# Sketched attention and four attention experts on one core: a new order for 1,270 jobs, the last group projected expert by expert

## The chip, the cores and the metric

One core of one Trainium2 chip runs the whole kernel in one launch. The metric is device time in microseconds (us). The engines are TensorE (PE, with its weight loads shown as PEld), VectorE (DVE), ScalarE (ACT), GpSimd (POOL) and SyncE (SP, which here only issues DMAs). Each has its own instruction queue, worked in program order; they meet through semaphores.

## The reference

Two blocks follow each other. The first is attention through sketches: for 4 batches, 4 heads, 1088 rows and 32 columns per head,

```
phi(x) = outer(S1 x, S2 x)                 # 8 x 8 = 64 features per row
kv = sum over rows of phi(k) v^T,  z = sum over rows of phi(k)
x  = phi(q) kv / (phi(q) z + 1e-6)         # joined over heads: 1088 x 128 per batch
```

The second is a mixture of four causal attention experts on x, two of which are chosen per row:

```
logits = x @ w_gate;  the two largest of 4 are kept, their softmax gives the shares w
for each expert e:  q, k, v = x wq[e], x wk[e], x wv[e]
                    a  = softmax(causal(q k^T / 8));  ye = a v wo[e]
out = sum over the two chosen experts of w * ye        # 4 x 1088 x 128, float32
```

## The kernel before

The weights are folded once: Mq[e] = wq[e] wk[e]^T / 8 and Mo[e] = wv[e] wo[e]. Then a row's scores are (x Mq[e]) x^T, and the output is (a x) Mo[e], so keys and values are x itself.

Each batch is prepared (`prepare`): k, q and v are loaded, k and q are turned in 32x32 blocks on DVE, multiplied with the sketch matrices on PE (L518), turned back on DVE (L522), and multiplied feature by feature on DVE or POOL (L527). PE sums features times v (L558, "sums"). Batch 0 goes by rows (`attend_rows`): its query features are transposed on PE (L592, "turn qf"), copied to SBUF ("keep qf"), multiplied with the sums (L615, "numer"), divided on DVE, and turned into xT. The other batches stay turned (`attend_turned`, L757). `choose_experts` computes logits (L807), compares them on DVE (L832 and on), and makes masks and shares; the masks of the first group of batch 0 are widened on PE (L906), all others go through DRAM (mb<-md). x goes through DRAM as well and comes back as rows (xra, xrb, xrc).

A batch's 1088 queries, twice over for their two chosen experts, are 17 tiles of 128 (64 queries x 2), in three groups of 6, 6 and 5 tiles. For a group: `queries` multiplies x with the four Mq (L960), and DVE picks the chosen expert's columns (L973). `scores` computes a tile's scores (L998, "score"), DVE masks and takes the maximum (L1010, "take"), ACT takes the exponential (L1026), POOL multiplies with share and inverse sum (L1041, "weigh"), and DVE turns the tile (L1046, "turn A"). `values` sums rows of x with these (L1074, "sum"), copies the sums ("keep V"), patches in the queries whose expert stands second (L1097, "patch"), and POOL multiplies two experts at a time with their masks (L1101, "spread V"). `outputs` projects with Mo (L1144; for groups of 5 tiles turned, L1124, with a turn-back on DVE, L1127), copies and stores. Batches 0 to 2 take their groups in the order 0, 1, 2, the last batch 1, 2, 0: the last group of the kernel is group 0 of batch 3.

What each engine does when is no loop order. Every step is a job with a name and one or two engines that may run it. The list `ORDER` names all jobs by number, with a letter where there is a choice of engine; `Plan.run` emits the jobs in that order and gives each buffer (a PSUM pair, a tile of a pool) to the job that asks first. So `ORDER` fixes every queue and every buffer. The costs and landing times in the job definitions were for whoever made the list: they change no instruction. Idle matmuls ("dummy", L247) are 40 jobs that may be emitted on PE, two matmuls each, or left out.

At the start the queues hold, before the change:

```
SP    w_gate, load S0, q, q, k, k, then v (4 pieces and 1 small), k of batch 1 (4), q of batch 1, the weights
ACT   q, load S1, q, the table, spread2, keep qf (5), keep sums (2), keep x
POOL  ident, mask, pick8, const, spread1, gate order, features q (2), spread v1, spread v0, features k of batch 1, rep4, ..., onehot, rep16
DVE   decode, spread3, turn q (2), turn k (2), back q (2), features q (2), back k (2), features k (4), turn k of batch 1, ...
PE    4 dummies, sketch q0, sketch k0, dummy, turn qf (5), sums 0 (2), sketch k1, numer (3), turn x, turn w (3), logits, ...
```

Of the kernel before, what the change touches and what calls it, by code (L numbers as in the profile page):

```python
# [14 lines left out]
ALU = mybir.AluOpType  # L15
# [6 lines left out]
56 45 47 0 1 8a 77 60 46 3 2 76 25a 19a 17a 48 79 49 51 78 57 90 89 74 87 75 88 50 13b 98 100 99 102a 103a 91 92 83 93  # L22
97a 84 81 104b 22a 101b 113 96a 117 118a 82 111 112a 115 109 110a 94a 95a 38b 80 392 86 85 106 116a 393 114a 105 108a
107a 391 394 402 395 401 405 406 119 404 408a 54 120 124 125 129 407 130 121 66 122a 52 64 58 53 65 146 131 410a 126
411a 67b 132a 400 127a 147 152 55 68 397 396 69 123 71 150 70 148 153 155 44b 398 180 72 27b 16b 684 149 151 167 168
169 170 63 156 157a 158 685 159a 59 409b 179 184a 183a 154 162 163 181 399 185 73 182 413 412 186 414a 61 403 174 687
686 695 694 416 194 62a 415 417 195 196 420b 418b 215 216 419b 217 218a 421 222 423 9b 24b 31b 26b 422 164 219 171 128
165 137 187 188 133 172 246 173 430 431 197a 198 223 424 425 189 190a 191 245 250a 12b 166a 199 688 249a 201 202 200
318 5b 432 160 203 208 175 251 7a 426 427a 433a 224 247 192 428b 248 225a 161a 209 429 434a 210 252 319 322a 323a 193
435 698 268 226 227 700 699 204a 205 206 139 220 135 176 267 269 270 228 436 438a 207 141 703a 271b 704b 437b 324 221  # L30
211a 212 260 261 262 263a 213 275 321 276 277 278 279b 177 178b 214 253 254 456 458 272 457 273 14b 142 693 320 325
255 292 291 293 274 701a 42b 264 691 280 702a 134 136 229 230 231 459 460 692 256b 234a 284 294 283 233a 462 281 257
232a 258 265 690 689 706 705 285 286 235b 342 707a 708 237 236 239 709 710 696 713a 238 711a 712a 259 282 697 461 266
295a 296 343 326 344 297 287a 327 328 288 289 298 714 715 717 463 350 290 329 330b 716 723 724 725 345 346a 10b 143
21b 472 138 331 473 477b 718 347 351 352 35b 353 354a 144 727a 332 348 719 140 29b 439 476b 464 299 300 301 302 303
304 308a 441 306a 307a 726a 333 349 467 478 335 310 474 440 334 305b 309 475 336 479 359 337 338a 358 360 339 361 362
355 468 508 509 442 720a 984 311 312 540 721a 363 340 501 364a 443 502 480 979 341 481 482 541 314 465 487 365 488 356
357 483a 315 313 366 367 538 494 977 978 495 980 316a 981 728 539 542a 368 369 370 987 496 503 504a 145 371 372 373
374 317 469 375 470 543a 544 545 471a 505 506 985 988 484 485 486 497b 444 498 722 499 510 511b 489 490a 491 512 513
376 379b 447 500 380a 515 383 516 553 377a 381 445 554 492 493 378a 382 448 584 585 586 517 518a 729 555 449 446 453  # L40
982 983 730a 514 519 731b 451 991 520 521 993 749 556b 992 994b 587 588a 569 546 996b 750 384 385 997a 507 557 558 547
751 548 386 568 989 522 589 523 524 549a 550 551 559 570 571 526a 752 753 590 242 591 525a 754 611 529 995a 530 241
528b 527a 531 612 616a 561 760 732 452 387 615a 755 455 466 733 572a 756 560 573 574 389 614 562 563 986 613 240 576
577 617 618 620 575 43b 552 532 644 28b 18b 619 578 579 621 243a 580b 581 643 765 652 564a 565 766 769a 582 651 768
757 645 583 636 566 567 390 653 770a 771 635 654 655 627 622 244 623a 761 762 628 637 656 657b 629 630 638 767 772 624
658 659 646 625 592 660 639a 640 631b 641 593 594 450 595 596 597 794 598a 999 647a 632 642 601b 602 648 600a 599a 795
633 634 649 998 736 1000a 603 605 535 626 454 773 774 787 650 534 763 788 533 780 781 808 809 810 811a 764a 536b 812
661 662 789 775 663 813 796 797b 798 790b 604 782 664 665 666 667 1002 814 668 669 990 1005a 734 776b 777 672a 671a
778 1006b 670b 1001 735 739 1003 832 1004a 791 388 799 783b 800 673a 674 675 831 835a 801 784 1007 802 803 1008 792
676 1009 793 836a 834 677 1010 1016 833 904 738 678 742 30b 758 804b 1011 837 1017 785 805 806 759 1012 1018 838 1013a  # L50
905 908a 862 1014a 1020a 909a 807 679 910 878 786 779 737 537 877 879 747 839 840 841 907 906 880 911 861 863 1019a
1021 881b 842a 846 847 682 740 815 816 817 746 864 865a 820a 853 866 867 821a 824 854 1015 868 882 936 819a 823 39b
34b 40b 41b 855 848 849b 937 818a 850 851 856 822 938 1022 1024b 869 1023b 607 843 883 884 939 870 748 871 872 1042
857b 1044 928 680 741 681 844 845 1043 858 606 873a 874 929 608 1045 825 1047 852 930 940a 1046 1048 875 859 860 921
944 945 946 920 743 941 609a 922 610 744 913 931 932a 1049 912 914 947 933 934 942 915 948 876 949 950b 1126 916a 917
951 1125 1053 918 1054 1124 1128b 935 1025 1127 923 952 885 886 943 887 888 889 890 1129a 1051 891a 1130 1131 892b
924a 925 894b 895 828 896 926 898 893a 33b 927 32b 826 953 827 1139 829a 830 4 1147 1140 919 897 1055 1146 1132 1133
1148 1154 1155 1156 1198 1199 1149 1150a 1197 1201a 1134 1052 1027 1141 1142b 1143 1200 954 955 956 957 958 959 1202a
745 1029 1028 1026 1035 683 1037 960 1056 1057b 1135b 1157 1158b 1159 961 962 1203 1204 1213 1136 1137 1170 963a 1144
1145 1160 966a 1161 1171 1214 964a 968 1151 1152 1138 965a 967 1237 1205 1206 1172 1173 1174a 1238 1229 1215 970 969  # L60
1031 1207 1208 1209a 1239 1216 1059 1153 1039 1230 1162 1163 1217a 1240 1058 1231 1164 1061 1210 1211 1165 1241 1060
1063b 1050 1218 1062b 1166b 971 1064 1167 1175 1232 1242 899 1212 972 1168 1065 1176 1177 6b 1233a 1234 1169 1221
1243b 1040 1244 1222 1223 901 1235 1224 1066 900 1038 1067 1068 1245 1246 1219 1033 1069b 902a 1032 1030 1220 1101
1102 973 1178 1179 1034 1087 1225b 1226 1227 1236 1073 1074 1180 1075 1228 1088 1076a 1036 1181 1080 1081 1077 1094
1095 1096 1182 1103 1104b 1183 1184b 1097b 1098 1186b 1089 1090b 1091 1247 1248 1249 976 1187a 1105 1106 1250 1251
1252 1041 1188 1253 1254 1255 1185b 1189 1092 11b 1190 23b 903 1107 36b 1191 1194 1078 1070 1082 1083a 1193 1099 1093
975 1084 1071 1257b 1100 974 1192 1258a 1256a 1079 1085 1260 1261 1263 1259b 1086 1262 1072 1108 1195a 1196 1109 1110
# [47 lines left out]
def kernel(  # L115
# [14 lines left out]
    nc = tc.nc  # L130
# [188 lines left out]
    def spread(e, h):  # L319
        copy(e, SK[32 * h : 32 * h + 32], SK[0:32])  # L320
# [913 lines left out]
```

## Time and profile before

| | us |
|---|---|
| median of 3 runs | 279.85 (279.17 to 280.01) |
| the profiled execution | 280.91 |
| its span | 279.2 |
| TensorE busy | 263.8 |
| VectorE busy | 218.8 |
| GpSimd busy | 153.3 |
| ScalarE busy | 100.2 |
| mean granted TensorE clock | 0.994 |

A matmul's end in the profile is modelled, and a pair of matmuls in float32 counts as two instructions, so a full PE row is not PE at its peak. The idle time of an engine counts only where the chain of work that ended last passes through it.

### The profile page before, as it was taken

Reading aid. Unit: us, or ns where it says so; the run is one execution under the profiler, and the core shown is the slowest. Engines: PE = TensorE matmul, PEld = TensorE weight load, DVE = VectorE, ACT = ScalarE, POOL = GpSimd, SP = SyncE. Lnnn points to the kernel's source line nnn. Section 1 sums busy time; section 2 is a strip of 40 time slices with the busy share of each in tenths; the row PEclk is TensorE's granted clock in tenths of the full one; section 3 lists DMA queues with packets and bytes.
Section 4 is the critical chain, followed back from the end, with each engine's and each line's share of the span. In section 5 each row is a group of like instructions: output and inputs, shape, how many; then the busy total and the mean of one; then the engine's idle time right before and its main releaser. Section 6 shows DMA issues by size and latency. Waiting matters only on the chain.

```text
span 279.2 us, 9471 instructions
## 1 busy us (share of the span) xinstructions
PE 263.8 (94%) x3953; PEld 194.8 (70%) x3953; DVE 218.8 (78%) x541; ACT 100.2 (36%) x272; POOL 153.3 (55%) x246
## 2 busy tenths in 40 slices
PE   5789899899999999989999999999999999999993
PEld 1478575448486796676589976756696975789973
DVE  4895998999989987998969437999898468986340
ACT  2030346254333444433462331463423335233110
POOL 6323636677789834546565458655447432544570
PEclk9979999999999999999999999999999999999999
DMA  8855749921617879243900166701403756820012
GB/s 179 139 141 102 112 124 258 153 34 24 143 32 120 166 184 180 57 102 65 198 6 4 30 150 141 162 2 38 108 2 76 130 116 133 165 56 5 2 31 52
DMA packets 85547, 27.36 MB, mean 98 GB/s; under 512 B 54080, under 2 KB 84864, under 8 KB 85504
## 3 DMA queue, kind: packets, MB, share of 16 engines
q1 hardware_dynamic: 83280, 26.47, 46.4%
q8 instruction: 31, 0.51, 0.8%
q10 hardware_dynamic: 2224, 0.28, 0.6%
q14 instruction: 12, 0.10, 0.1%
HBM read 22.22 MB, written 4.52 MB: 96 GB/s over the span
## 4 chain that ended last, share of the span: by engine, by line
PE 70%; DVE 20%; issue 5%; POOL 2%; ACT 1%; DMA 1%; DVEq 0%; POOLq 0%
PE pair L1074 24%; PE pair L998 19%; PE pair L960 9%; PE pair L1144 6%; PE pair L518 3%; PE pair L558 3%; DVE AT L1046 2%; DVE w L522 2%; DVE w L1010 2%; DVE fp L527 2%; PE pair L1124 2%; PE pair L615 1%; PE pair L592 1%; DVE in L494 1%; DVE xT L191 1%
## 5 line engine op out<-in xcount | busy, mean ns | idle before, releaser
L1041 POOL TENSOR_SCALAR w<-w,rs,sh 128x384 f32<-128x384 f32 (+15 forms) x68 | 55.6, 824 | 54.8 <-DVE rs L1037 52.0
L998 PE MATMUL pair<-xT,qs 128*128 128x384 f32 (+11 forms) x216 | 76.8, 482 | 1.7 <-DVE agg L191 1.3
L1026 ACT ACTIVATE w<-w,mx 128x640 f32<-128x640 f32 (+15 forms) x68 | 52.4, 770 | 72.3 <-DVE mx L1010 56.6
L998 PEld LDWEIGHTS pair<-xT,qs 128*128 128x128 f32 x216 | 37.7, 190 | 26.9 <-issue 10.0
L1046 DVE STREAM_TRANSPOSE AT<-w 128x576 f32<-128x576 f32 (+13 forms) x68 | 50.6, 758 | 5.4 <-POOL w L1041 5.2
L1010 DVE CUSTOM_DVE_ANT_0 w<-pair,mask 128x768 f32<-128x768 f32 (+13 forms) x68 | 48.3, 721 | 5.4 <-PE pair L998 4.7
L1074 PEld LDWEIGHTS pair<-AT,xra 32*128 32x128 f32 x1136 | 41.6, 185 | 6.0 <-DVE mx L1010 2.6
L1074 PE MATMUL pair<-AT,xra 32*128 32x192 f32 (+5 forms) x1136 | 44.5, 303 | 0.0
L1101 POOL TENSOR_TENSOR agg<-agg,mb 128x768 f32<-128x768 f32 (+1 forms) x24 | 37.3, 1565 | 12.7 <-ACT agg L191 6.6
L960 PE MATMUL pair<-xT,Mq 128*128 128x384 f32 (+1 forms) x96 | 34.9, 478 | 0.1
L527 POOL TENSOR_TENSOR fp<-w 128x576 f32<-128x576 f32 x21 | 25.4, 1224 | 14.2 <-DVE w L522 12.5
L191 ACT COPY agg<-pair 128x384 f32<-128x384 f32 (+1 forms) x33 | 14.0, 462 | 44.2 <-PE pair L1074 37.7
L1074 PE MATMUL pair<-AT,xrb 32*128 32x160 f32 (+5 forms) x752 | 26.9, 287 | 0.3 <-issue 0.3
L1074 PEld LDWEIGHTS pair<-AT,xrb 32*128 32x128 f32 x752 | 26.1, 186 | 1.0 <-issue 1.0
L1144 PEld LDWEIGHTS pair<-Mo,agg 128*128 128x128 f32 x192 | 23.4, 192 | 4.1 <-POOL agg L1101 1.7
L1144 PE MATMUL pair<-Mo,agg 128*128 128x128 f32 x192 | 24.9, 279 | 1.0 <-POOL agg L1101 0.9
L960 PEld LDWEIGHTS pair<-xT,Mq 128*128 128x128 f32 x96 | 17.2, 190 | 11.2 <-issue 3.2
L973 DVE COPY_PREDICATED qs<-mb,pair 128x768 f32<-128x768 uint16 (+1 forms) x24 | 23.0, 960 | 2.4 <-DMA mb<-md 1.8
L191 DVE COPY agg<-pair 128x384 f32<-128x384 f32 (+1 forms) x15 | 7.9, 532 | 13.1 <-PE pair L1074 11.7
L518 PE MATMUL pair<-in,SK 32*32 32x288 f32 x416 | 13.4, 494 | 3.0 <-DVE in L494 3.0
L522 DVE STREAM_TRANSPOSE w<-pair 128x576 f32<-128x576 f32 x16 | 11.6, 756 | 5.6 <-PE pair L518 5.6
L1097 DVE COPY_PREDICATED agg<-mb,pair 128x384 f32<-128x384 uint16 (+1 forms) x24 | 12.6, 550 | 3.3 <-ACT agg L191 2.9
(160 smaller groups left out, 295.4 us busy)
## 6 DMA issues: line engine op xcount, KB each, us to landing
mb<-md SPq DMA_DIRECT2D x7, 576.0 KB, 5.2
xra<-xd SPq DMA_DIRECT2D x16, 192.0 KB, 4.3
xrb<-xd SPq DMA_DIRECT2D x16, 192.0 KB, 3.6
xrc<-xd SPq DMA_DIRECT2D x16, 160.0 KB, 4.9
mb<-md SPq DMA_DIRECT2D x4, 480.0 KB, 5.4
in<-in_k_dram SPq DMA_DIRECT2D x12, 136.0 KB, 4.1
in<-in_q_dram SPq DMA_DIRECT2D x3, 544.0 KB, 5.5
xd<-w SPq DMA_DIRECT2D x12, 136.0 KB, 3.5
```

The source lines that it names most:

```text
L191: (nc.scalar.copy if eng == "ACT" else VEC[eng].tensor_copy)(o, i)
L527: VEC[e].tensor_tensor(out=f, in0=a[:, :, None, R : 2 * R].to_broadcast([128, NJ, R, R]), in1=a[:, :, 0:R, None].to_broadcast([128, NJ, R, ...
L960: nc.tensor.matmul(plan[ps[x]][:, y, 0:w], Mq[:, ((1, 2), (0, 3))[x][y]], plan[xT][:, 64 * t0 : 64 * t1], start=True, stop=True)
L973: nc.vector.copy_predicated(chosen(), rows(c), rows(plan[ps[x]]))
L998: nc.tensor.matmul(plan[p][:, y, 0 : c1 - c0], plan[qs][:, 128 * t : 128 * t + 128], plan[xT][:, c0:c1], start=True, stop=True)
L1010: nc.vector.tensor_tensor_reduce(out=o, in0=src, in1=msk, scale=-1.0, scalar=mx[:, b, i, x - 1 : x] if x else 3e38, op0=ALU.add, op1=ALU.m ...
L1026: nc.scalar.activation(out=a, in_=a, func=ACTF.Exp, bias=mx[:, b, i, last : last + 1], scale=-1.0, accum_out=zs[:, b, i : i + 1])
L1041: nc.gpsimd.tensor_scalar(out=a, in0=a, scalar1=rs[:, b, i : i + 1], scalar2=plan[("sh", b)][:, i : i + 1], op0=ALU.mult, op1=ALU.mult)
L1046: nc.vector.transpose(dst[:, 0 : keys // 32, t], plan[A][:, 0:keys].rearrange("p (j s) -> p j s", s=32))
L1074: nc.tensor.matmul(plan[Vk[g // 2]][:, g % 2, lo : 32 * nt], plan[(f"xr{j // 12}", b)][rows, j % 12], a[rows, j, lo:], start=(j == 0), sto ...
L1101: nc.gpsimd.tensor_tensor(out=a, in0=a, in1=plan[mb][:, 2 * x : 2 * x + 2, 0:w], op=ALU.mult)
L1144: nc.tensor.matmul(plan[p][0:m, 0, 128 * x : 128 * x + 128], plan[agg][:, e, 128 * x : 128 * x + m], Mo[:, e], start=(e == 0), stop=(e == ...
```

## The change

1. `spread v` (the copy that brings batch 0's v into its padded tile) may run on ScalarE or POOL. In the new order the small piece (v1, 64x128) runs on ScalarE and the large one (v0, 128x1024) stays on POOL.
2. `spread2` on ScalarE follows the table load.
3. The last group (batch 3, group 0) has its own way in `values` and `outputs`: experts 0 and 1 are multiplied with their masks straight from PSUM on DVE ("mix"), experts 2 and 3 are kept, patched, and scaled one by one on POOL or DVE ("scale"), PE projects expert by expert as they come (order 0, 2, 1, 3) into three pieces in two PSUM pairs, and each piece is copied and stored by itself.
4. Nine dummies stand ahead of the first sketch instead of four; the two later ones are gone, and one stands behind the last projection.
5. All jobs have a new order. At the start:

```
SP    q, load S0, q, k, v, k, w, v, w, w, v, v, v small, k of batch 1, wo, w_gate, k of batch 1 (3), q of batch 1
ACT   load S1, q, q, the table, spread2, spread v1, keep w, keep qf (3), keep x, ...
POOL  mask, const, spread1, rep16, ident, pick8, features q (2), spread v0, rep4, gate order, onehot, features k of batch 1 (2), ...
DVE   decode, turn q (2), spread3, turn k (2), back q (2), features q (2), back k (2), features k (4), keep qf, keep sums (2), ...
PE    9 dummies, sketch q0, sketch k0, turn w (3), turn qf (4), sums 0 (2), turn qf, numer (3), turn x, sketch k1, logits, ...
```

The diff, with the lists cut out and the changed cost and landing figures of loads left out:

```diff
 ORDER = """
...
-    job("table", "ACT", 1.5, lambda e: nc.scalar.activation(out=warm, in_=warm, func=ACTF.Exp), ["room"], rank=-150)
+    job("table", "ACT", 1.5, lambda e: nc.scalar.activation(out=warm, in_=warm, func=ACTF.Exp), ["room"], "table", rank=-198)
...
-        job(f"spread{h}", ("DVE", "POOL", "ACT")[h % 3], (0.12, 0.2, 0.22)[h % 3], lambda e, h=h: spread(e, h), ["ST"], "SKW", rank=-189)
+        job(f"spread{h}", ("DVE", "POOL", "ACT")[h % 3], (0.12, 0.2, 0.22)[h % 3], lambda e, h=h: spread(e, h), ["ST"] + (["table"] if h == 2 else []), "SKW", rank=-189)
...
-        def spread_v(x):
+        def spread_v(e, x):
             if x == 0:
-                nc.gpsimd.tensor_copy(plan[vp][:, 0:N8, :, 0:D].rearrange("p j h d -> p h j d"),
+                copy(e, plan[vp][:, 0:N8, :, 0:D].rearrange("p j h d -> p h j d"),
...
-                job(f"spread v{x}", "POOL", 1.2 if x == 0 else 0.3, lambda e, x=x: spread_v(x), [("vl", b)], ("vp", b),
+                job(f"spread v{x}", ("ACT", "POOL"), (0.95, 1.2) if x == 0 else (0.3, 0.3), lambda e, x=x: spread_v(e, x), [("vl", b)], ("vp", b),
...
+        if last_group(b, n):
+            def mix(x):
+                nc.vector.tensor_tensor(out=by_half(plan[agg][:, x]), in0=sums_of(x), in1=by_half(plan[mb][:, x]), op=ALU.mult)
+
+            def scale_one(e, x):
+                a = plan[agg][:, 2 + x, 0:w]
+                VEC[e].tensor_tensor(out=a, in0=a, in1=plan[mb][:, 2 + x, 0:w], op=ALU.mult)
+
+            for x in range(2):
+                job(f"keep V {b}.{n}.{2 + x}", ("ACT", "DVE"), (a_us(w), d_us(w)), lambda e, x=x: keep(e, 2 + x),
+                    [("V", b, n)], ("aggk", b, n, 2 + x), [Vk[x], agg], rank=r)
+                job(f"mix V {b}.{n}.{x}", "DVE", d_us(w), lambda _, x=x: mix(x), [("V", b, n), *masks_of(b, n, 0)], ("agg", b, n, x),
+                    [Vk[x], agg, mb], rank=r + 0.01 * x)
+                job(f"patch V {b}.{n}.{x}", "DVE", d_us(w), lambda _, x=x: patch(x),
+                    [("V", b, n), ("aggk", b, n, 2 + x), *masks_of(b, n, 2)], ("aggp", b, n, x), [Vk[1 - x], agg, mb], rank=r + 0.01)
+                job(f"scale V {b}.{n}.{x}", ("POOL", "DVE"), (p_us(w), d_us(w)), lambda e, x=x: scale_one(e, x),
+                    [("aggp", b, n, x), *masks_of(b, n, 1)], ("agg", b, n, 2 + x), [agg, mb], rank=r + 0.02)
+            return
...
+        if last_group(b, n):
+            ps = [("ps", "po", b, n, x) for x in range(2)]
...
+            def project_expert(e, first_, last_):
+                for x in range(3):
+                    nc.tensor.matmul(piece(x), plan[agg][:, e, 128 * x : 128 * x + 128], Mo[:, e], start=first_, stop=last_)
...
+            order = (0, 2, 1, 3)
+            for y, e in enumerate(order):
+                job(f"out {b}.{n}.{e}", "PE", 12 * 0.056, lambda _, e=e, y=y: project_expert(e, y == 0, y == 3),
...
+            for x in range(3):
+                job(f"keep out {b}.{n}.{x}", ("ACT", "DVE"), (a_us(128), d_us(128)), lambda e, x=x: keep_piece(e, x),
+                    [("po", b, n, 3)], ("ob", b, n, x), [ps[x // 2], ob], rank=rank + 0.01 + 0.001 * x)
+                job(f"store out {b}.{n}.{x}", ("SP", "ACT"), (0.45, 0.45), lambda e, x=x: store_piece(e, x), [("ob", b, n, x)], None, [ob],
+                    landing=0.37, rank=rank + 0.01 + 0.001 * x)
+            return
```

In the new order the queues of the last group are: DVE keep V 2, mix 0, patch 0, patch 1, turn out of group 2, mix 1, scale 1, three copies of output pieces; ACT keep V 3, then two of the three stores; POOL both products of group 2, then scale 0; PE the sums, group 2's projection, then experts 0, 2, 1, 3.

More of the change, by code (lines that the diff above doesn't have):

```diff
@@ L27 @@
[L27 to L36, printed above, removed]
@@ L465, in prepare @@
             for x in range(4):
-                job(f"load q{b}.{x}", "ACT" if x % 2 else "SP", 0.8, lambda e, x=x: by_head(nc.scalar if e == "ACT" else nc.sync, plan[qin], q, x),
-                    lead, ("qin", b), [qin], landing=0.95, rank=rank(-0.09))
+                job(f"load q{b}.{x}", "ACT" if x % 2 else "SP", 0.42, lambda e, x=x: by_head(nc.scalar if e == "ACT" else nc.sync, plan[qin], q, x),
+                    lead, ("qin", b), [qin], landing=0.85, rank=rank(-0.09))
         else:
```

102 lines of the change are left out of this document (62 added, 40 removed).

## The prediction

> **What bounds the kernel now.** I read the page first, then busy time by stretch, then the chain of work in order of time, and last the timeline at both ends.
>
> ```profile
> PE 263.8 (94%) x3953; PEld 194.8 (70%) x3953; DVE 218.8 (78%) x541; ACT 100.2 (36%) x272; POOL 153.3 (55%) x246
> ```
>
> ```profile
> 0.00:20.00 20.00, 14.16 (x179) 7.99 (x180) 15.26 (x39) 3.38 (x6) 9.27 (x30) 0.91 0.76 160
> ...
> 60.00:80.00 20.00, 20.00 (x322) 13.03 (x318) 18.59 (x54) 8.60 (x25) 13.69 (x20) 1.00 0.32 68
> ...
> 140.00:160.00 20.00, 20.00 (x449) 18.50 (x451) 13.28 (x34) 8.06 (x25) 10.70 (x13) 1.00 0.05 12
> ...
> 260.00:279.00 19.00, 14.41 (x241) 12.84 (x233) 5.28 (x13) 2.57 (x6) 7.81 (x8) 1.00 0.13 31
> ```
>
> The rows give the stretch, then busy time (and instructions) of PE, PE's weight loads, DVE, ACT and POOL, then TensorE's granted clock, the DMA share and GB/s. Three regimes show. From 60 to 80 DVE is the full engine (18.59 of 20). From 140 to 160 it has slack (13.28) and TensorE sets the pace, with the most matmuls of these stretches (449). In the first 20 us and the last 19 neither is full: there a chain of single steps sets the time, and there the change edits code. The chain at the start:
>
> ```profile
> 1.25 2.41 DMA w<-in_S_dram
> ...
> 7.93 2.61 PE pair L518 x64
> ...
> 12.04 2.82 DVE fp L527 x2
> ...
> 16.28 2.79 PE pair L592 x12
> 19.07 2.55 PE pair L558 x72
> 21.62 1.53 PE pair L518 x63
> 23.16 4.16 PE pair L615 x36
> ...
> 29.89 0.42 DVE ch L832
> 30.31 1.41 DVE ch L833
> ```
>
> These are: the sketch matrices land, the first query sketch (L518), feature products (L527) behind its turn back, transposes (L592), key sums (L558), the sketch of the next batch's keys (21.62), the numerators (L615), and the choice of experts on DVE.
>
> **The early part, step by step.**
>
> ```profile
> 1.31 3.59 PE L247 MATMUL pair<-idle 128*128 128x512 bf16 x8 [1.31 <-DVE idle L240]
> ```
>
> ```profile
> 12.90:16.30 3.40, 1.90 (x9) 1.00 0.67 131
> 16.30:19.70 3.40, 3.40 (x26) 0.51 0.73 196
> 19.70:23.10 3.40, 3.40 (x129) 0.99 0.02 5
> ```
>
> The second fence gives stretches of 3.4 us with TensorE's busy time and granted clock. Idle matmuls before the first sketch go from 8 to 18. The eight took 0.449 us each and never sped up; then TensorE idled to 7.93 and the sketch took 2.61 us, where the same 64 matmuls took 1.53 at 21.62 with full clock. A half-busy stretch (1.90 of 3.40) was followed by one at clock 0.51, and a full stretch of 3.40 us by 0.99. After the change TensorE is busy without a hole from 1.31 to about 7.9, 6.6 us, nearly twice that stretch, so I expect a warm sketch: 1.53 for 2.61, -1.1. Against it: if all 18 ran slow they would last 18 x 0.449 = 8.1, to 9.4, and delay the sketch by 1.5. Bounds -1.1 and +1.5; I take -0.8, near the warm end, since one stretch was enough in the rows above.
> [...]
>
> ```profile
> 11.43 2.83 POOL L527 TENSOR_TENSOR fp<-w 128x576 f32<-128x576 f32 x2 [4.41 <-DVE w L522]
> 12.04 2.82 DVE L527 TENSOR_TENSOR fp<-w 128x576 f32<-128x576 f32 x2
> 14.20 0.81 POOL L452 COPY vp<-w 64x128 f32<-64x128 f32 x1
> ...
> 16.26 2.77 DVE L527 TENSOR_TENSOR fp<-w 128x576 f32<-128x576 f32 x4
> 25.20 1.27 POOL L346 COPY rep<-ident 32x128 f32<-32x128 f32 x4
> 30.22 1.46 POOL L370 CAST AT<-ident 64x1536 bf16<-64x1536 f32 x1
> ```
>
> The key features: two on DVE beside POOL's products took 1.41 each, four without POOL 0.69 each. In the new order POOL runs the identity copies (L346, 1.27) and the one-hot cast (L370, 1.46) right after the large v copy, so they fall beside the four key features, where POOL was free. Cost: 0 if copies do not slow DVE, up to 2 x (1.41 - 0.69) = 1.4 if two of the four are slowed; I take +1.2, because under that same cast the small compare L833 took 1.41 us of the chain. The features then end at 19.03 - 0.8 + 1.2 = 19.4. [...]
>
> The sums: before, they waited for the slow transposes (to 19.07), not for the features. Now the first half starts on two features and the second follows at 19.4: 36 matmuls at half of 2.55 end at 20.7 for 21.62. The sketch of the next keys (1.53) moves behind the numerators, so these start at 20.7 + 0.45 (two copies of the sums, now DVE) = 21.15 for 23.16: -2.0. Behind the numerators the sketch stands before the logits (+1.5), and DVE gets a turn and a turn-back ahead of the compare (0.7 each) while the weights' copy (0.95) leaves it for ScalarE. The compare starts at about 29.0 for 29.89. The cast no longer meets it, but two feature products of the next batch do on POOL; I count these as equal. **Early: -0.9**, bounds +1.5 (cold clock) and -2.5 (warm, no collision).
>
> ScalarE takes only the small v piece (0.81 us on POOL); the order leaves the large copy on POOL. This adds a wait to ScalarE's queue:
>
> ```profile
> w<-in_v_dram SPq DMA_DIRECT2D x2, 16.0 KB, 4.2
> ...
> 4.51 0.91 SPq L439 DMA_DIRECT2D w<-in_v_dram  x2
> ```
>
> The small piece's load, issued at 4.51 before, now stands last of v on SP, behind three weight loads and behind the landing of a key load that itself waits for the first query load: about 4.2 for each, so an estimate of 8.5, issue 8.7, landing 12.9. Behind it on ScalarE are the weights' copy and three copies of turned query features, whose buffers the transposes and sums wait for. That is about 1.8 us of work, done at 14.7, covered by the features until two are ready near 17.9: cost 0; past 16 every us of late landing is a us on the sums. The loads of S swap places (S1 now ahead of a query load on ScalarE, S0 behind one on SP): 0, at most a few tenths, since the landing took 2.41 behind such a load already.
>
> **The middle.**
>
> ```profile
> L191 DVE COPY AT<-pair 128x768 f32<-128x768 f32 x1 | 0.9, 949 | 0.0
> L191 DVE COPY qs<-pair 128x384 f32<-128x384 f32 x5 | 2.7, 537 | 0.0
> ```
>
> All orders change. I counted DVE's queue ahead of the last transposed A of batch 0, where TensorE takes over. The old order has there two feature products (1.4), the weights' copy (0.95), two query copies (1.1) and small pieces (1.2) that the new one lacks; the new one has about 2.5 us that the old one lacks: 2.1 less. Ahead of the same point of batch 1's first group the new order has about 2.4 more. The one pulls TensorE's phase earlier, the other eats slack. Bounds -2.1 and +2.4; I take **-0.5**, nearer to nothing.
>
> **The last group.**
>
> ```profile
> 264.97 2.76 POOL L1101 TENSOR_TENSOR agg<-agg,mb 128x640 f32<-128x640 f32 x2 [3.19 <-issue]
> 265.67 3.18 PE L1074 MATMUL pair<-AT,xra 32*128 32x192 f32 x92
> 268.78 2.42 PE L1124 MATMUL pair<-agg,Mo 128*128 128x320 f32 x8
> 268.91 1.02 DVE L191 COPY agg<-pair 128x384 f32<-128x384 f32 x2 [3.30 <-PE pair L1074]
> 269.61 3.30 POOL L1101 TENSOR_TENSOR agg<-agg,mb 128x768 f32<-128x768 f32 x2 [1.88 <-ACT agg L191]
> 270.04 1.06 DVE L1097 COPY_PREDICATED agg<-mb,pair 128x384 f32<-128x384 uint16 x2
> 271.24 0.52 DVE L1127 STREAM_TRANSPOSE ob<-pair 128x320 f32<-128x320 f32 x1
> 272.96 2.50 PE L1144 MATMUL pair<-Mo,agg 128*128 128x128 f32 x20 [0.95 <-POOL agg L1101]
> 275.54 0.48 ACT L191 COPY ob<-pair 128x384 f32<-128x384 f32 x1 [5.76 <-issue]
> 276.04 0.39 SPq L1157 DMA_DIRECT2D out_dram<-ob  x1
> ```
>
> POOL's two wide products (1.65 each, to 272.9) hold the last 20 matmuls. New queue on DVE after the sums end at 268.85: keep 0.51, mix, two patches at 0.53 each, then the other group's turn-back (0.52, not before 271.2), then mix 0.53 and scale. Not shown is a product of 384 columns: DVE between 0.69 x 384/576 = 0.46 and a patch's 0.53, I take 0.5; POOL between 0.82 (half of 768) and 0.92 (768 and 640 columns differ by 0.25 of 1.65), I take 0.9. So DVE reaches the end of its scale at 271.7 + 1.05 = 272.8. TensorE, at 0.125 a matmul (2.50/20), does four experts of 6: from 271.25, 272.0, 272.75, 273.5 to 274.25. Three copies of 128 columns (at most 0.3 each) end near 275.2, with the last store issued then for 276.04: -0.85. Three stores of 64 KB for one of 192 KB on two queues: -0.25, bounds 0 and the 0.4 between these rows:
>
> ```profile
> out_dram<-ob SPq DMA_DIRECT2D x2, 192.0 KB, 2.1
> out_dram<-ob SPq DMA_DIRECT2D x4, 40.0 KB, 1.7
> ```
>
> Ahead of it, DVE now does seven jobs (3.0 us) between group 2's sums (262.8) and the last transposed A, so the last sums start near 265.9 for 265.67: +0.2. POOL's products of group 2 swap order and end near 268.2, before their matmuls at 268.78: 0. **Tail: -0.9**, bounds 0 (the turn-back stands ahead of mix and scale, and one us of lateness there is one at the end) and -1.5.
>
> **Sum.** -0.9 - 0.5 - 0.9 = -2.3 on the profiled execution's 280.91 (span 279.2 and 1.7 around it), 278.6. That execution is 1.06 above the median 279.85, so against runs I forecast 277.6. About 0.3% (0.84 us) is what a measurement of this kernel can tell from no change.
>
> **Rivals.**
> - Better: no collision on the key features and a warm clock, so that the early part gives its whole -2.5, the rest as forecast (-1.4): 279.85 - 3.9 = 276.0. For it: four features took 2.77 with POOL free. Against: POOL is not free there.
> - The idle matmuls stay slow: the sketch starts at 9.4, still slow, and ends at 12.0 for 10.5, which is +1.5 where the sum has -0.8: 277.6 + 2.3 = 279.9, no change to be told. For it: none of the eight in the trace sped up. Against: the stretch at 16.3, after which the clock came back.
> - The tail does not do what it says, because the other group's projection comes late and mix and scale stand behind its turn-back: +0.9, 278.5.
> - Slower: in the DVE-bound stretch new neighbours on POOL slow two-input work on DVE. One such meeting cost between 1.0 and 1.4 us (the compare L833: 1.41 in the chain, the compare before it 0.42); I take 1.3. The forecast gain is gone with two more meetings on the path, and three give 277.6 + 3.9 = 281.5. For it: DVE is 93% busy there, so nothing hides it; POOL is 68% busy. Against: the old order has such meetings too.
>
> **How the numbers follow.** Forecast 0.36 (its own range 275.5 to 279.0), better 0.20, slow idle matmuls 0.11, lost tail 0.07, slower 0.26. Faster by over 0.3%: forecast, better and lost tail, less 0.03 of the forecast's upper end: 0.60. Within: 0.11. Slower: the fourth rival and that 0.03, 0.29. The range runs from 274.4 (the better rival with the middle's -2.1 in full for -0.5) to 282.3 (the slower one, three meetings, with the last group giving 0.1 for 0.9); what lies outside is four meetings and more, and gains in the middle beyond the count.
>
> **What would show it.** Right: a first sketch of some 1.5 us; key features above 0.69 each beside the two POOL copies; numerators from about 21; the compare near 29; the last store issued about 9.3 us after the last sums start (265.67 to 276.04 is 10.4 now). Wrong: a sketch that starts after 9; the small v copy on ScalarE after 16; DVE idle by more than a tenth between 60 and 80; last sums that start later than 266.

## The result: slower by half a per cent, and the profile after

The changed kernel takes 281.87 us (median of 23 runs) beside 279.85 for the kernel before: a ratio of 1.0048, interval 1.003 to 1.0065. The forecast was 277.6. The time lies inside the range on record, 274.4 to 282.3, but on the other side of no change. Some executions of each of these kernels are disturbed and longer; the ratios here leave them out and the medians do not, and as the execution recorded with the result was such a one (span 289.5 us), the lines of the changed kernel below come from an ordinary one, recorded with the experiments (282.24 us, span 280.5). Line numbers are one higher than before's up to the sums of a group, and more behind them.

Busy time by stretch, columns as in the prediction (PE, weight loads, DVE, ACT, POOL, clock, DMA share, GB/s), changed kernel:

```profile
60.00:80.00 20.00, 20.00 (x349) 12.98 (x328) 19.45 (x44) 9.02 (x21) 13.71 (x19) 1.00 0.59 122
...
100.00:120.00 20.00, 18.52 (x410) 13.83 (x402) 15.02 (x35) 7.26 (x22) 10.88 (x19) 1.00 0.35 75
120.00:140.00 20.00, 18.93 (x152) 13.26 (x153) 16.72 (x42) 6.62 (x15) 10.81 (x11) 0.91 0.53 105
```

The same two middle stretches of the kernel before:

```profile
100.00:120.00 20.00, 20.00 (x438) 15.10 (x434) 17.60 (x43) 7.05 (x21) 9.53 (x16) 1.00 0.67 118
120.00:140.00 20.00, 18.68 (x109) 12.37 (x106) 18.40 (x43) 8.31 (x21) 10.46 (x17) 1.00 0.60 125
```

From 60 to 80 DVE is as full as before (19.45 for 18.59), and TensorE is busy throughout at full clock in both, so the stretch that I feared is no worse. From 100 to 140 DVE works 4.3 us less. TensorE stands for 1.5 us from 100 to 120, where it did not stand before, and from 120 to 140 its clock is 0.91.

The chain of work at the start of the changed kernel, and TensorE's first rows:

```profile
2.01 6.28 DMA in<-in_q_dram
8.41 0.13 DVE in L495
...
22.53 4.23 PE pair L616 x36
...
30.40 0.37 DVE ch L833
...
34.48 1.13 DVE ch L834
```

```profile
1.31 6.51 PE L248 MATMUL pair<-idle 128*128 128x512 bf16 x18 [1.31 <-DVE idle L241]
9.84 3.39 PE L519 MATMUL pair<-in,SK 32*32 32x288 f32 x128 [2.02 <-DVE in L495]
```

One line of DVE's waits (us in total, times, longest):

```profile
DVE in L495 <- DMA in<-in_q_dram: 3.2, 1, 3.2
```

The chain now begins with a load of queries that lands at 8.3, where it began with the sketch matrices. The sketch starts at 9.84 for 7.93, the compare near 30.4 for 29.89.

The chain at 111 us, TensorE's row behind it, SP's own queue there, and that stretch (columns as above):

```profile
111.33 1.37 POOL agg L1102
112.72 7.22 DMA mb<-md
120.06 0.88 DVE qs L974
```

```profile
121.07 3.34 PE L1146 MATMUL pair<-agg,Mo 128*128 128x320 f32 x8 [2.55 <-DVE qs L974]
```

```profile
102.49 1.82 SPq L788 DMA_DIRECT2D xra<-xd  x2
112.72 0.38 SPq L898 DMA_DIRECT2D mb<-md  x1
...
113.74 0.46 SPq L788 DMA_DIRECT2D xra<-xd  x1
```

```profile
112.00:128.00 16.00, 13.45 (x242) 8.89 (x213) 9.87 (x23) 5.88 (x17) 8.17 (x9) 0.89 0.53 110
```

SP stands from 104.3 to 112.72 in front of one fetch of masks (batch 1, last group). The three mask buffers are all in use; the oldest is free when GpSimd's product for batch 0's last group ends at 112.7. The fetch then takes 7.22 us. On TensorE, the queries of that group stand ahead of the projection L1146 and hold its PSUM until the mask select at 120.06; TensorE stands 2.55 us for it. Behind the fetch, on the same queue, stand gathers of x (xra, xrb) for the next sums. The clock in this stretch is 0.89: (1 - 0.89) x 16 is 1.8 us of full speed, on top of the wait.

The last group of the changed kernel:

```profile
268.63 3.18 PE L1075 MATMUL pair<-AT,xra 32*128 32x192 f32 x92
...
274.00 2.84 PE L1172 MATMUL pair<-Mo,agg 128*128 128x128 f32 x24
...
276.88 0.69 DVE L192 COPY ob<-pair 128x128 f32<-128x128 f32 x3 [1.26 <-PE pair L1172]
277.24 1.00 ACTq L1178 DMA_DIRECT2D out_dram<-ob  x2
277.39 0.36 SPq L1178 DMA_DIRECT2D out_dram<-ob  x1
```

From the start of the last sums to the end of the span it takes 280.5 - 268.63 = 11.9 us, where it took 279.2 - 265.67 = 13.5. So the coded part does better than forecast, and it starts three us later. Where the three us were lost is seen from a mark in between, the sums of batch 0's second group, here in the kernel before and in the changed one:

```profile
78.46 4.18 PE L1074 MATMUL pair<-AT,xra 32*128 32x192 f32 x96
```

```profile
78.33 4.18 PE L1075 MATMUL pair<-AT,xra 32*128 32x192 f32 x96
```

They start level (the forecast had the changed kernel 0.9 ahead). From there to the last sums it is 265.67 - 78.46 = 187.2 us before and 268.63 - 78.33 = 190.3 in the changed kernel: the middle is 3.1 us longer. In four traces with the old order, the kernel before and three of the runs below, it takes 186.5 to 187.2. The start of this mark differs by 0.5 us between traces of the same instructions, so sizes in the early part are no finer than that.

### The profile page after: what moved, and what is told of

Read it like the earlier page. It is cut to its first block, busy times and chain, and to the rows that moved or that the text cites. A ratio compares the mean times of both kernels' runs of the same rounds, so it can differ in the third digit from the quotient of the medians.

```text
span 289.5 us, 9489 instructions
## 1 busy us (share of the span) xinstructions
PE 273.8 (95%) x3961; PEld 203.2 (70%) x3961; DVE 219.6 (76%) x551; ACT 100.5 (35%) x270; POOL 154.9 (53%) x240
## 4 chain that ended last, share of the span: by engine, by line
PE 71%; DVE 14%; DMA 4%; issue 3%; POOL 3%; ACT 2%; SPq 1%; DVEq 0%; POOLq 0%
PE pair L1075 25%; PE pair L999 18%; PE pair L961 7%; PE pair L1196 6%; PE pair L1146 4%; PE pair L519 3%; DMA mb<-md 3%; PE pair L616 3%; DVE qs L974 2%; PE pair L559 2%; DVE w L523 2%; POOL agg L1102 2%; DMA in<-in_k_dram 2%; DVE AT L1047 2%; DVE w L1011 1%
## 5 line engine op out<-in xcount | busy, mean ns | idle before, releaser
L1042 POOL TENSOR_SCALAR w<-w,rs,sh 128x256 f32<-128x256 f32 (+14 forms) x68 | 55.9, 827 | 51.5 <-DVE rs L1038 49.5
L1027 ACT ACTIVATE w<-w,mx 128x64 f32<-128x64 f32 (+16 forms) x68 | 52.4, 770 | 72.2 <-DVE mx L1011 64.2
L1047 DVE STREAM_TRANSPOSE AT<-w 128x64 f32<-128x64 f32 (+16 forms) x68 | 50.9, 760 | 5.6 <-POOL w L1042 5.6
L1011 DVE CUSTOM_DVE_ANT_0 w<-pair,mask 128x512 f32<-128x512 f32 (+15 forms) x68 | 47.8, 721 | 4.3 <-PE pair L999 3.1
L1075 PE MATMUL pair<-AT,xra 32*128 32x160 f32 (+5 forms) x1136 | 45.5, 310 | 0.0
L1102 POOL TENSOR_TENSOR agg<-agg,mb 128x768 f32<-128x768 f32 (+1 forms) x22 | 34.2, 1566 | 15.5 <-DVE agg L1098 6.9
L528 POOL TENSOR_TENSOR fp<-w 128x576 f32<-128x576 f32 x24 | 28.4, 1202 | 17.7 <-DVE w L523 16.7
L1196 PE MATMUL pair<-Mo,agg 128*128 128x128 f32 x168 | 21.4, 277 | 0.1
L1038 DVE RECIPROCAL rs<-rs 128x1 f32<-128x1 f32 x68 | 9.1, 141 | 11.2 <-ACT rs L1033 9.0
L1035 POOL TENSOR_SCALAR rs<-zs 128x1 f32<-128x1 f32 x24 | 5.1, 214 | 22.9 <-ACT w L1027 20.7
```

The costliest lines, as they stand in the source:

```text
L528: VEC[e].tensor_tensor(out=f, in0=a[:, :, None, R : 2 * R].to_broadcast([128, NJ, R, R]), in1=a[:, :, 0:R, None].to_broadcast([128, NJ, R, ...
L1011: nc.vector.tensor_tensor_reduce(out=o, in0=src, in1=msk, scale=-1.0, scalar=mx[:, b, i, x - 1 : x] if x else 3e38, op0=ALU.add, op1=ALU.m ...
L1027: nc.scalar.activation(out=a, in_=a, func=ACTF.Exp, bias=mx[:, b, i, last : last + 1], scale=-1.0, accum_out=zs[:, b, i : i + 1])
L1042: nc.gpsimd.tensor_scalar(out=a, in0=a, scalar1=rs[:, b, i : i + 1], scalar2=plan[("sh", b)][:, i : i + 1], op0=ALU.mult, op1=ALU.mult)
L1047: nc.vector.transpose(dst[:, 0 : keys // 32, t], plan[A][:, 0:keys].rearrange("p (j s) -> p j s", s=32))
L1075: nc.tensor.matmul(plan[Vk[g // 2]][:, g % 2, lo : 32 * nt], plan[(f"xr{j // 12}", b)][rows, j % 12], a[rows, j, lo:], start=(j == 0), sto ...
```

## The experiments

Every ratio is to the kernel before, measured beside it on the same chip. Diffs that move jobs in the list are given by job names.

**The parts by themselves.** The changed kernel again, for a profile and as the mark for the others:

> The changed kernel itself, to see where an ordinary execution loses its time. Clock theory (the new order makes TensorE lose its full clock for more stretches of 3.4 us than the old one): granted clock near 0.98 where the old order has 0.994, the numerators (36 matmuls, 4.16 us before) at 6 to 8 us, median 281 to 282. Load theory (queries land late, the first sketch starts late): first sketch after 9 us for 7.93. Middle theory: DVE waits for masks or TensorE waits for DVE's picks between 60 and 140, several us in all.

281.66 us, ratio 1.0052 (1.0021 to 1.0084). Of the signs named, the late sketch (9.84) and the mask wait that lasts to 120 are there. The numerators take 4.23 us, not the 6 to 8 of a cold clock.

Before's order up to the last sums, then the new last group:

```diff
 order: before, up to the last "sum 3.0.x"
-keep, patch, spread V 3.0; out 3.0; one store
+keep, mix, patch, scale V 3.0; out 3.0.0, .2, .1, .3; three stores
```

> The old order up to the end of the last sums, then the changed last group (expert by expert). Forecast of the tail: 0.9 to 1.1 us less than before, 278.8 to 279.0. Rival (the other group's turn-back holds up mix and scale): no change, 279.7 to 280.1.

277.92 us, ratio 0.9912 (0.9894 to 0.9931). The last sums of this kernel:

```profile
264.49 3.18 PE L1075 MATMUL pair<-AT,xra 32*128 32x192 f32 x92
```

Its span ends at 276.2, 11.7 us after the sums' start, 1.8 less than before. The runs say 2.5 (0.88% of 280); the traces account for 1.8 of it.

```diff
 PE, order: before
-4 dummies, sketch q0, sketch k0, dummy, ...
+9 dummies, sketch q0, sketch k0, dummy, ...
```

> The old order with nine idle jobs (18 matmuls) ahead of the first sketch for four. Forecast of that step: the first sketch in about 1.5 us for 2.6, and 0.5 to 1.1 less in time, 278.8 to 279.4. Rival (they run slow and delay the sketch): first sketch later than 8.5, time 280.5 or more. Clock theory adds: if the clock that is won early is lost at the same place as before, the gain stays; if it moves the loss onto the sums and numerators, no gain.

279.42 us, ratio 0.997 (0.9952 to 0.9989): 0.8 us gained, what the forecast had for a warm first sketch. The two sketches take 3.19 us in its trace, for 4.95 before.

So the two parts that were edited bring about 3.3 us, and the kernel with both is 1.4 slower. The new order of everything else costs some 4.7.

**Is it the clock?** Six more idle matmul jobs, after the turns of the weights:

```diff
 PE, order: after
-turn w2, turn w1, turn w0, turn qf (3), ...
+turn w2, turn w1, turn w0, 6 dummies, turn qf (3), ...
```

> The changed kernel with six more idle jobs (12 matmuls) behind the transposes of the weights, where TensorE waits for the query features. Clock theory: the stretch from 13 to 16.6 is full now, the clock is kept, numerators near 4.2 us, mean clock 0.99 or more, time 2 to 5 us less than the changed kernel, and fewer far-off executions. Load and middle theories: within 1 us of the changed kernel.

281.3 us, ratio 1.0021 (0.9993 to 1.0049), not told apart from the changed kernel's 1.0052. A cold clock in the time before the numerators is at most a small part. The jobs don't touch the stretch from 33 to 48, where the clock is below full in this run as well (0.78).

**The wait for masks, first try.** A fourth mask buffer:

```diff
-        "mb": several("mb", 3, [128, 6, GW], BF16),
+        "mb": several("mb", 4, [128, 6, GW], BF16),
```

> The changed kernel with four buffers for the expert masks in place of three, nothing else. In the trace of the changed kernel the fetch of the masks for the last group of batch 1 is issued at 112.72 us, right when the multiply that reads the oldest of the three buffers ends on GpSimd; it lands 7.22 us later, the mask select runs at 120.06, and TensorE has been idle for 2.55 us by then, with the clock at 0.89 from 112 to 128. Theory (the wait for the buffer makes most of the loss in the middle): the fetch is issued near 104, no wait for masks is left on TensorE there, the clock is 1.00 from 112 to 128, and the time falls by 2.0 to 2.9 us, to 278.8 to 279.7, no longer slower than the kernel before. Rival 1 (the loss comes from the first 50 us, and the wait at 117 only stands where a wait would come anyway, for VectorE's backlog): less than 0.7 us is gained, 281.0 to 281.7. Rival 2 (the transfers that are issued earlier meet the gathers of x and hold up the sums): a gain at 117 and a loss of the same size behind it, 281.5 or more.

283.67 us, ratio 1.0116 (1.0077 to 1.0154): slower still. The wait did go: the sums of batch 1 start at 120.28 for 125.48, and the clock from 112 to 128 is 1.00. Then, in the chain:

```profile
139.20 5.78 PE pair L1075 x140
144.99 1.68 issue
146.66 1.54 PE pair L1075 x37
148.20 3.98 PE pair L559 x72
```

TensorE stops for 1.68 us in the middle of sums, waiting for nothing that the profile shows, and the key sums after it take 3.98 us for 2.22. With four buffers SP ran ahead and fetched two sets of masks (576 KB each) at 135.7 and 136.8. In this run the same sums began at 139.2, in the changed kernel at 144.57. The DMA queues between 143.7 and 143.8 in this run, and between 145.7 and 145.8 in the changed kernel (queue, kind: packets that start in that tenth of a us, MB, the time that these packets take as a share of 16 engines' tenth of a us; it runs on beyond the tenth, so it does not say how full the engines are):

```profile
q1 hardware_dynamic: 32, 0.01, 97.6%
q8 instruction: 1, 0.02, 94.6%
```

```profile
q8 instruction: 1, 0.02, 93.3%
q1 hardware_dynamic: 48, 0.03, 89.9%
```

The next load of instructions (q8) came about 4.5 us after these sums began, for 1.2 in the changed kernel, where it started beside a q1 about as busy. So the traffic of that tenth is not what sets the two apart, and why the load came late is not shown. Whether the early mask fetch made the stop was tested by moving the second mask fetch behind the gathers for batch 2:

```diff
+        "mb": several("mb", 4, [128, 6, GW], BF16),
 SP, order: after
-..., fetch masks 2.0, fetch x 1.22, fetch masks 2.1, fetch x 1.23, ...
+..., fetch masks 2.0, fetch x 1.22, fetch x 1.23, store out, fetch x 2.0 (3), store out, fetch masks 2.1, ...
```

> The changed kernel with four mask buffers, and the fetch of the masks for the middle group of batch 2 moved on SP's queue behind the gathers for batch 2, so that it is not issued at 136.75 us any more. With four buffers alone, two mask fetches of 576 KB each kept the DMA engines busy from 135 to 144.5; the load of instructions for the sums that began at 139.2 came at 143.7 (in the changed kernel 1.2 us after the sums' start), and TensorE stood still from 144.99 to 146.66 with nothing in the profile to wait for, and lost its clock. Theory (the early fetch held up the load of instructions): the stop at 145 goes, the clock stays at 1.00 from 128 to 200, and 2.5 to 5 us less than the 283.7 of four buffers alone are left: 278.5 to 281. Rival (the stop has another cause): TensorE stops in the same sums again and the time stays at 283 or more.

282.21 us, ratio 1.0062 (1.0031 to 1.0093). In its chain the stop is gone, the same sums run in one piece, and the load of instructions comes 2.0 us after their start:

```profile
138.62 7.04 PE pair L1075 x174
145.66 2.22 PE pair L559 x72
```

That agrees with the late load of instructions as the cause of the stop, on one trace of each kernel. The two ratios differ by 0.5%, but their intervals overlap. The time missed the 278.5 to 281 that I expected: the profiled execution took 280.32 and most others more. What those lost is not shown, and I leave it open.

**Second try, by order alone.** The last group's queries of batch 1 behind the sums, as the kernel before has them:

```diff
 PE and DVE, order: after
-numer 2, query 1.2 (4), score 1.9, logits 2, pick 1.2 (2), out 0.2, ..., sum 1.0 (3), score 1.10, out 0.0, ...
+numer 2, score 1.9, logits 2, out 0.2, ..., sum 1.0 (3), score 1.10, out 0.0 and query 1.2 (4) in turn, pick 1.2 (2), ...
```

> The changed kernel with the query matmuls of batch 1's last group, their two copies by ScalarE and their two mask selects moved behind the first group's sums of batch 1, as the kernel before has them, with three mask buffers as they are; nothing else. In the changed kernel these queries hold PSUM banks ahead of the product with the output weights (L1146), and the banks come free only with the mask select at 120.06 us. Theory (the order of these few jobs makes the loss in the middle): the product no longer waits, the sums of batch 1 start 4 to 5 us earlier, TensorE's clock is 1.00 from 112 to 128, and of this 2.5 to 5 us reach the end: 276.7 to 279.2. Rival (as in the run with four buffers, where TensorE stood 5.3 us ahead at 122 us and lost it again between 141 and 157): the wait goes and the time stays at 281 or more.

286.6 us, ratio 1.019 (1.0141 to 1.0239). That is the rival's side, but neither theory had the reason. TensorE's rows in the sums, and SP's:

```profile
122.41 0.60 PE L1075 MATMUL pair<-AT,xra 32*128 32x192 f32 x6 [2.53 <-DMA xra<-xd]
124.27 4.81 PE L1075 MATMUL pair<-AT,xra 32*128 32x192 f32 x86 [1.26 <-DMA xra<-xd]
```

```profile
112.40 0.38 SPq L898 DMA_DIRECT2D mb<-md  x1
...
113.42 0.46 SPq L788 DMA_DIRECT2D xra<-xd  x1
```

With the masks out of TensorE's way, it waits for what stood behind them on SP: 3.8 us for two gathers. The wait for masks had covered this one. By itself the queries' move cost time. The place to mend is SP's queue. So, with the queries as in the last run:

```diff
 SP, order: after
-fetch masks 1.2, fetch x 1.12, fetch x 1.00, store out, fetch x 1.11, fetch x 1.03, ...
+fetch x 1.12, fetch x 1.00, store out, fetch x 1.11, fetch x 1.03, fetch masks 1.2, ...
```

> The changed kernel with batch 1's last queries and mask selects behind the first sums of batch 1, and with the fetch of that group's masks behind the gathers of x on SP's queue; three mask buffers, nothing else. In the run with the queries moved alone, TensorE waited 3.8 us in those sums for gathers that SP issued at 113.4 to 117, behind the mask fetch that waited for GpSimd until 112.4. Theory (one place on SP's queue makes the loss in the middle): the gathers are issued near 105, TensorE waits for neither masks nor gathers from 112 to 128, and the time falls to 277 to 279.5. Rival (a later limit takes its place): no wait there, and 281 or more at the end.

278.88 us, ratio 0.9964 (0.994 to 0.9988). SP's rows, TensorE's sums, and the stretch:

```profile
106.19 0.47 SPq L788 DMA_DIRECT2D xra<-xd  x1
...
112.81 0.38 SPq L898 DMA_DIRECT2D mb<-md  x1
```

```profile
120.23 3.18 PE L1075 MATMUL pair<-AT,xra 32*128 32x192 f32 x92
```

```profile
112.00:128.00 16.00, 15.12 (x274) 11.21 (x243) 12.24 (x30) 7.61 (x22) 10.58 (x12) 1.00 0.46 88
```

The fetch is issued when it was before (112.81 for 112.72), and no engine waits for it now. 1.0052 to 0.9964 is 2.5 us: one job's place on SP, together with the queries' place. The fetch moved alone was not run, so what it would bring without the queries is open.

**The first queries.**

```diff
 ACT, order: after
-load S1, load q0.3, load q0.1, table
+load q0.1, load S1, load q0.3, table
 SP
-q0.0, S0, q0.2, k0.1, v0.3, k0.0, w2, v0.0, ...
+q0.0, S0, q0.2, k0.1, k0.0, v0.3, v0.0, w2, ...
```

> The changed kernel with three loads moved: on ScalarE's queue the second query load goes ahead of the second sketch table, and on SP's queue the first load of values and the first weights go behind the second half of the keys; nothing else. In the trace of the changed kernel ScalarE's two query loads land 5.3 us after their issue (3.2 in the kernel before), VectorE waits 3.2 us for them until 8.41, and the sketch of the queries starts at 9.84 (7.93 before). Theory (late queries cost what the early part does): the sketch starts by 8.7, the compare of the first gate near 29.7 in place of 30.9, and the time falls by 0.8 to 1.2 us, to 280.5 to 280.9. Rival (the lateness is made up before the first scores, since TensorE's work stands level again near 20 us): the time changes by less than 0.4 us, 281.3 to 282.1.

280.25 us, ratio 1.0006 (0.998 to 1.0033): 1.3 us less than the changed kernel, the expected 0.8 to 1.2 within what the intervals allow. The run moves loads on ScalarE's and on SP's queue together, so it does not tell which of the two counts. ScalarE's two query loads (KB each, us to landing) in the kernel before, in the changed kernel and in this one, and the sketch of this one:

```profile
in<-in_q_dram ACTq DMA_DIRECT2D x2, 136.0 KB, 3.2
```

```profile
in<-in_q_dram ACTq DMA_DIRECT2D x2, 136.0 KB, 5.3
```

```profile
in<-in_q_dram ACTq DMA_DIRECT2D x2, 136.0 KB, 4.0
```

```profile
8.77 3.38 PE L519 MATMUL pair<-in,SK 32*32 32x288 f32 x128 [0.57 <-DVE in L495]
```

**Both mends.** The earlier loads with the queries of group 1.2 moved, but with the mask fetch still ahead of the gathers:

```diff
 PE, DVE: as in the run with the queries moved
 ACT, SP: as in the run with the first queries ahead
```

> The changed kernel with the queries of batch 1's last group behind the sums, and with the first queries' loads ahead again, nothing else. If the two losses are separate they add up: 1.3 us less than the run with the moved queries alone, 275.4 to 277.9, level with the old order with the nine idle matmul jobs and the new tail (277.1) or better. If both only move the work up to one later limit, the second mend brings less than 0.5 us.

Its times scatter too far for a ratio (281.58 to 287.55). Its profile has the wait for gathers again (4.0 us), which fits the run without the early queries. And with the gathers ahead as well:

```diff
 SP, order: the run above
-fetch masks 1.2, fetch x 1.12, fetch x 1.00, store out, fetch x 1.11, fetch x 1.03, ...
+fetch x 1.12, fetch x 1.00, store out, fetch x 1.11, fetch x 1.03, fetch masks 1.2, ...
```

> The same with the first queries' loads ahead again. If the early loss and the loss in the middle are separate and are all that the new order loses: 1.3 us below the run with the gathers moved alone, 275.7 to 278.2, level with or below the old order with nine idle jobs and the new tail (277.1). If they hide one another: less than 0.5 us below it.

277.58 us, ratio 0.9902 (0.9864 to 0.9939), 1.7 us below the run with the gathers alone. The first sketch, the sums of batch 0's second group and the last sums:

```profile
8.19 3.06 PE L519 MATMUL pair<-in,SK 32*32 32x288 f32 x128
```

```profile
76.19 4.18 PE L1075 MATMUL pair<-AT,xra 32*128 32x192 f32 x96
...
263.53 3.18 PE L1075 MATMUL pair<-AT,xra 32*128 32x192 f32 x92
```

The two losses add up: 1.5%, 4.2 us, lie in two places, the load queues at the start and the mask fetch with the queries of its group. That the time meets the forecast of 277.6 is luck in part. By the traces this kernel is 2.3 us ahead of before at the sums of batch 0's second group (forecast 0.9), level in the middle (187.3 us for 187.2; forecast 0.5 shorter), and 1.2 shorter from the last sums to the end (12.3 us for 13.5; forecast 0.9).

**The sketch of the next keys, ahead of the numerators again.**

```diff
 PE, DVE, POOL, order: after
-numer 0 (3), divide 0 (3), turn x, sketch k1, ..., back k1 (2), ..., onehot, features k1 (4)
+sketch k1, back k1.0, features k1 (2), numer 0 (3), divide 0 (3), back k1.1, features k1 (2), ..., onehot
```

> The changed kernel with the sketch of batch 1's keys, its two copies back and its four feature products ahead of the numerators and the choice, about as in the kernel before; nothing else. In the trace of the changed kernel GpSimd makes those products from 33.25 to 35.56 us, and one product of the choice on VectorE (L834) takes 1.13 us in that stretch for 0.19 in the kernel before; the first scores start at 39.25 with TensorE idle for 1.3 us ahead of them, and the clock is 0.77 from 33 to 48. Theory (the move of the sketch behind the numerators, which I counted as a gain, costs more than it brings, by the collision): the product of the choice takes 0.2, the first scores start 0.5 to 1.2 us earlier, the clock from 33 to 48 is 1.00, and the time falls by 0.8 to 2.0 us, to 279.7 to 280.9. Rival (my forecast's step): the numerators start 1.2 to 1.5 us later, the choice with them, and the time stays or rises by up to 1.2 us, 281.7 to 282.9.

283.79 us, ratio 1.0135 (1.009 to 1.018), and no verdict on the move: the keys of batch 1 are loaded later in the new order, so the sketch waited for them (1.9 us), and the numerators behind it took 7.67 us for 4.23 (they took 7.95 at a granted clock of 0.50, from 23 to 33 us, in the execution recorded with the result). One thing it does show. Without feature products beside it on POOL, a product of the choice takes 0.19 us, not 1.13:

```profile
40.80 0.19 DVE L834 TENSOR_TENSOR ch<-ch 128x22 f32<-128x22 f32 x1
```

**A version that beats both.** Before's order, nine idle jobs, the new last group:

```diff
 order: before, up to the last "sum 3.0.x"
-4 dummies ahead of sketch q0
+9 dummies ahead of sketch q0
-keep, patch, spread V 3.0; out 3.0; one store
+keep, mix, patch, scale V 3.0; out 3.0.0, .2, .1, .3; three stores
```

> The order of the kernel before up to the end of the last sums, with nine idle matmul jobs ahead of the first sketch, and then the last group expert by expert: the two parts of the change that helped by themselves (ratios 0.9912 and 0.997 to the kernel before), without the rest of the new order. If the two add up: 277.0 (276.6 to 277.5), a ratio of 0.986 to 0.990. If the tail alone already had the good clock at the start: 277.9, a ratio of 0.991.

277.12 us, ratio 0.9903 (0.9875 to 0.993), where the two parts alone multiply to 0.988. Together with the mended new order (0.9902) it is the fastest here; the two can't be told apart. So the idle jobs and the new last group are enough for the whole gain, and no run shows one from the rest of the new order. Measured against this run, the rest cost the changed kernel 1.0052 - 0.9903 = 1.5%, 4.2 us, as much as the two mends gave back.

## Why the prediction was wrong, step by step

Two steps failed. The larger is the middle, forecast at -0.5, which came out at +2.5 by the runs and +3.1 by the traces: DVE's queue was counted, and SP's load queue was not walked. The other is the early part, where the moved loads were priced at nothing: 1.3 to 1.7 us. The last group was right in kind, and sized too small.

- **The early part, -0.9.** The step that failed is one that the text does not have: it takes the sketch from "busy without a hole from 1.31 to about 7.9" and never asks when the queries land. It weighed the loads of S ("0, at most a few tenths") and the late small v piece, and left out that the same swaps put ScalarE's query loads behind S1 and beside a load of values and of weights. They took 2.1 us longer from issue to landing (5.3 for 3.2), DVE waited 3.2 us, and the sketch started 1.9 us late. Cost: 1.3 us in the one pair of runs, 1.7 in the other. The rest of the step stood: the idle matmuls sped up (18 in 6.51 us) and gave 0.8 by themselves, the two sketches took 3.39 us for 4.95, and with the queries and the gathers mended the sketch starts at 8.19.
- **In that step, the key features, +1.2.** They are hardly slowed by POOL's copies: four took 2.99 us beside them, for 2.77 without. It is POOL's copies that took longer, 2.14 for 1.27:

```profile
17.06 2.99 DVE L528 TENSOR_TENSOR fp<-w 128x576 f32<-128x576 f32 x4
```

```profile
16.63 2.14 POOL L347 COPY rep<-ident 32x128 f32<-32x128 f32 x4
```

- **Numerators at 21.15, compare at 29.0.** They came at 22.53 and 30.4. The 1.9 us of the late sketch are enough for it. The 7.85 us between the two came true (7.87), but the terms that I named for that step do not add up to it, so the number held without a working. Two products of the choice were stretched (1.07 and 1.13 us) beside the feature products that I counted "as equal", where the kernel before has one (1.41). TensorE stands 1.3 us before the first scores, and the clock from 33 to 48 is 0.77, in the mended kernel too. What that costs in time is open, since the run that should have told failed for another reason.
- **The middle, -0.5, bounds -2.1 and +2.4.** It was sized by counting DVE's queue alone. The loss came over SP's queue, which the prediction didn't walk: +2.5 by the runs, at the upper bound, and +3.1 by the traces, above it. One mask fetch at the head of that queue waited 8.4 us for its buffer, with gathers behind it. The order of fetches and gathers around each group is part of a new order, and a fetch that needs a buffer back is a wait for whoever frees it, here GpSimd until 112.7.
- **The last group, -0.9.** Right in kind and too small: 1.7 us in the changed kernel by the traces, 1.8 to 2.5 with the old order. The three copies took 0.69 us together where I had "at most 0.3 each". From the last copy to the end of the span it is 2.9 us (2.8 in a trace with the old order) for 3.2 with one large store, so the smaller stores are worth about the 0.25 forecast. The last sums follow the projection without a gap, so the 0.2 for seven jobs on DVE did not come.
- **The rivals.** The slower one gave 281.5, near the 281.87, but by collisions between DVE and POOL in the stretch from 60 to 80. That stretch shows no loss, so its time was met by another mechanism. The signs named beforehand did point right: a sketch after 9 (9.84) and last sums after 266 (268.63) were two of the four that were to prove the forecast wrong.

## What to carry to other kernels

When an order is redone, walk the load queues as carefully as the engines': for each load, when it is issued, what stands ahead of it, and what it must wait for before it can be issued. Here a load that waited for a buffer at the head of SP's queue held back every load behind it: SP stood for 8.4 us, from 104.3 to 112.7, with gathers behind that were needed. Put behind such a load only what is needed later. And when a wait is taken away, look for what it covered: here a second wait, 3.8 us for gathers, stood behind the first, 2.55 us for masks.

## What the runs showed of the hardware

- A stop of TensorE of 1.3 us was followed by a granted clock of 0.51. The first scores of the changed kernel, and the stretch around them (columns as above):

```profile
39.25 0.43 PE L999 MATMUL pair<-xT,qs 128*128 128x64 f32 x2 [1.30 <-DVE qs L974]
```

```profile
33.00:48.00 15.00, 13.55 (x181) 8.82 (x181) 11.33 (x39) 5.30 (x18) 7.47 (x20) 0.77 0.64 133
```

  The clock is 0.51 from 40.4 to 47.3; over the stretch that is (1 - 0.77) x 15 = 3.5 us of full speed. The length of the stop alone doesn't decide: the kernel before has a stop of 1.37 us there, and keeps a clock of 1.00 from 33 to 48. What decides is open.

```profile
33.73 0.82 PE L906 MATMUL pair<-cTa,AT 64*128 64x192 bf16 x8 [1.37 <-DVE ch L811]
```

- A load of instructions came late in one run. With four mask buffers one (16 KB, on q8) started about 4.5 us after the sums began, for 1.2 in the changed kernel and 2.0 with the second fetch moved. There TensorE stopped for 1.68 us, and the key sums behind took 3.98 us for 2.22. That the load made the stop is argued from one trace of each; the wait itself is in no row.
